# Attention scores multiplied once, with the exponentials turned by DMA, in a kernel of block attention and Fourier mixing

## The chip, the cores and the metric

The kernel runs on one core of one Trainium2 chip. The metric is the time of one execution on the device in microseconds, the median of several runs. The core's engines work side by side, each through its own queue in order: PE (TensorE, matrix products), DVE (VectorE), ACT (ScalarE), POOL (GpSimd) and SP (SyncE, which here only issues DMAs). An instruction that needs another engine's result waits at the head of its queue, and all behind it wait too.

## What is computed

Inputs are q, k and v (4 batches, 8 heads, 768 positions, head size 64), a small matrix per head, and two MLP weights. The small matrix is normalised to P (8x8); it mixes the eight blocks of 96 positions of k and of v. Then attention runs within each block, and its output goes through a two-dimensional Fourier transform, a layer norm and an MLP:

```python
k_sorted = einsum('bhij,bhjcd->bhicd', P, k_b)      # v_sorted likewise
scores = scale * matmul(q_b, k_sb.transpose(0, 1, 2, 4, 3))   # 96x96 per block
scores = scores - max(scores, axis=-1, keepdims=True)
attn = exp(scores)
attn = attn / (sum(attn, axis=-1, keepdims=True) + 1e-09)
x = matmul(attn, v_sb)                    # heads side by side: (4, 768, 512)
u = x + real(fft(fft(x, axis=1), axis=2))
un = (u - mean(u)) / sqrt(var(u) + 1e-06)
out = u + maximum(un @ w_ch1, 0) @ w_ch2
```

## The kernel before

**Order.** The program is written as steps, each with the engines that can do it and a cost in ns, the buffers that it reads and writes, and a priority. A planner (`Plan`, L166 to L301) sorts them before the program is built: time and again it takes, among the steps that could start within 40 ns of the earliest, the one of the highest priority, gives it to an engine (`"V"` DVE, `"A"` ACT, `"T"` PE, `"G"` POOL, `"S"` SP) and counts on with the stated costs. `hop` is the time from the end of a DMA's issue to its landing. The order of each queue on the chip is the one planned; the chip's own waits come on top. Buffers come from rings with a fixed number of tiles, and a step can only be planned when its buffers are free. In a `chain` the first step waits until the buffers of all of its steps are there. Earlier batches come before later ones, and MLP steps come last of all (priority 1e6 and more), so MLP matmuls fill what PE has left.

**One batch.** `mix(b)`: casts and sums v, multiplies k and v by P (`k_mix`, whose result is copied into `kzs`, and `v_mix`), transposes q into `qT`, and moves the mixed v by DMA into `vs`, one row of partitions per position of a block (`v_move`, 12 DMAs from SP). Then attention, head by head in two halves of four blocks. Then `post(b)`: the Fourier transform's second part, the residual, its store to HBM (`store_u`, SP), statistics, normalisation and transposition. Then `mlp(b, gr)` for two groups of 384 positions: 64 matmuls into the hidden layer (L924), a relu on ACT for each four of them (L930), 48 matmuls back (L945), a load of u from HBM (`load_u`, SP) and the sum (L952).

**One half of attention**, the part that the change touches. `maxima` (L651) multiplies scores with queries on partitions (L661, four matmuls) and takes the row maximum on DVE (L664) into `mxs`. `scores` (L667) multiplies them again, turned, with keys on partitions: four matmuls put minus the maximum into the bank (L676, `nident` is minus the identity), four add keys times queries (L680); ACT takes the exponential of all 96x384 at once (L685) into `sm`. `minus_one` (L688) subtracts one and rounds to float16 into `eT` (DVE or ACT). `values` (L700) multiplies `eT`, whose 97th row is all ones, by `vs`, whose 97th row holds the share of the ones and the column sums (L708), and divides by the last column (L713, L714, DVE). Rings: `mxs` 6, `sm` 4, `eT` 3, one `eT` for both halves of a head.

**Start.** `junk` (L451) holds ones for warm-up matmuls and for clearing `kzs`; `lm` (L490) takes a constant that SP loads later.

Of the kernel before, what the change touches and what calls it, by code (L numbers as in the profile page):

```python
# [9 lines left out]
F32 = mybir.dt.float32  # L10
F16 = mybir.dt.float16
AF = mybir.ActivationFunctionType
ALU = mybir.AluOpType
AX = mybir.AxisListType

B = 4
H = 8
S = 768
# [286 lines left out]
def kernel(  # L305
# [30 lines left out]
    def ring(tag, n, shape, dtype):  # L336
        plan.rings[tag] = Ring([const.tile(shape, dtype, name=f"{tag}{i}") for i in range(n)])
# [8 lines left out]
    ring("vg", 1, [128, H, D], F32)  # L346
    ring("kron", 2, [128, H, 16, NB], F16)
    ring("qT", 4, [128, S], F16)
    ring("mxs", 6, [BLK, 4], F16)
    ring("sm", 4, [BLK, 4, BLK], F32)  # L350
    ring("rz", 4, [BLK, 4], F32)
    ring("xs", 2, [BLK, 4, 128], F16)
    ring("x4", 2, [BLK, 2, 2, 128], F16)
# [10 lines left out]
    ring("ur", 2, [128, DM], F32)  # L364
    ring("outt", 2, [128, DM], F32)
    ring("mh", 1, [128, 2, 2 * LT], F16)
    plan.rings["eT"] = Ring([const.tile([97, NB, BLK], F16, name=f"eT{i}") for i in range(3)])
    eTs = plan.rings["eT"].tiles

    def bank(b, shape, dtype=F32):  # L370
        n = int(np.prod(shape[1:]))
        t = b.t if dtype == F32 else b.t.bitcast(dtype)
        t = t[0:shape[0], 0:n]
        if len(shape) == 3:
            t = t.rearrange("p (a c) -> p a c", c=shape[2])
        return t
# [71 lines left out]
    mask8 = const.tile([64, NB], F32, name="mask8_sb")  # L448
    nc.sync.dma_start(mask8, mask8_d.ap())
    selj = const.tile([64, 128], F32, name="selj_sb")  # L450
    junk = const.tile([128, DM], F16, name="junk")  # L451
    nc.vector.memset(junk, 1.0)
    ident = const.tile([128, 128], F16, name="ident")
    nc.vector.memset(ident, 0.0)
# [32 lines left out]
    negm = const.tile([128, 1], F32, name="negm_sb")  # L487
    idx = const.tile([128, 6 * B], mybir.dt.uint32, name="idx_sb")
    rsel = const.tile([BLK + 3, 2, BLK + 1], F16, name="rsel_sb")
    lm = const.tile([128, 2, 2, 385], F16, name="lm_sb")  # L490

    xr2 = [const.tile([BLK + 3, NB, DM], F16, name=f"xr{i}") for i in range(2)]
    w1sb = const.tile([128, 4, DFF], F16, name="w1sb")
# [107 lines left out]
    def k_mix(b, hp, gh):  # L601
        pK = Buf("bank")

        def f(e):
            k4 = k16[b, hp].t.rearrange("p h (g d) -> p h g d", d=D)
            ps = bank(pK, [128, 3, 128])
            for g in range(3):
                for hh in range(2):
                    nc.tensor.matmul(
                        ps[64 * hh:64 * hh + 64, g, :], k4[:, hh, 3 * gh + g, :],  # L610
                        kron[b].t[:, 2 * hp + hh].rearrange("p c i -> p (c i)"))

        def ev(e, hh):
            r = slice(64 * hh, 64 * hh + 64)
            dst = kzs[hp][r, hh].rearrange("x (i g c) -> x i g c", g=G, c=16)
            copy(e, dst[:, :, 3 * gh:3 * gh + 3, :],
                 bank(pK, [128, 3, 128])[r].rearrange("x g (c i) -> x i g c", c=16), SCALE)
        plan.chain(("psK", b, {"T": 360}, f, [k16[b, hp], (kron[b], hp // 2)], [pK]),
                   *[("kz", b, {"A": 484, "V": 551}, lambda e, hh=hh: ev(e, hh), [pK],
                      [("kz", hp, hh, gh)]) for hh in range(2)])  # L620
# [30 lines left out]
    def maxima(n, half):  # L651
        b, h = divmod(n, H)
        hp, hh = h // 2, h % 2
        mxs[n, half] = Buf("mxs")
        pS = Buf("bank")

        def f(e):
            ps = bank(pS, [BLK, 4, BLK])
            for j in range(4):
                col = slice(BLK * (4 * half + j), BLK * (4 * half + j + 1))  # L660
                nc.tensor.matmul(ps[:, j, :], qT[b, hp].t[:, col], kzs[hp][:, hh, col])  # L661
        plan.chain(
            ("psS", b, {"T": 185}, f, [qT[b, hp]] + [("kz", hp, hh, g) for g in range(2)], [pS]),
            ("max", b, {"V": 548}, lambda e: nc.vector.tensor_reduce(  # L664
                mxs[n, half].t, bank(pS, [BLK, 4, BLK]), axis=AX.X, op=ALU.max), [pS], [mxs[n, half]]))

    def scores(n, half):  # L667
# [5 lines left out]
        def f(e):  # L673
# [4 lines left out]
            for j in range(4):  # L678
# [6 lines left out]
            ("exp", b, {"A": 487}, lambda e: nc.scalar.activation(  # L685
                sms[n, half].t, bank(pS, [BLK, 4, BLK]), AF.Exp), [pS], [sms[n, half]]))

    def minus_one(n, half):  # L688
        if half == 0:
            eT[n] = Buf("eT")  # L690

        def f(e):
            dst = eT[n].t[0:BLK, 4 * half:4 * half + 4, :]
            if e == "A":
                nc.scalar.add(dst, sms[n, half].t, -1.0)  # L695
            else:
                nc.vector.tensor_scalar(dst, sms[n, half].t, -1.0, None, op0=ALU.add)
        step("minus", n // H, {"V": 459, "A": 518}, f, r=[sms[n, half]], w=[(eT[n], half)])

    def values(n, half):  # L700
        b, h = divmod(n, H)
        pN, rz = Buf("bank"), Buf("rz")

        def f(e):
            ps = bank(pN, [BLK, 4, D + 1])
            for j in range(4):
                i = 4 * half + j
                nc.tensor.matmul(ps[:, j, :], eT[n].t[:, i, :],  # L708
                                 vs[2 * (b % 2) + h // 4][:, i, (D + 1) * (h % 4):(D + 1) * (h % 4 + 1)])

        def g(e):
            ps = bank(pN, [BLK, 4, D + 1])
            nc.vector.reciprocal(rz.t, ps[:, :, D])  # L713
            nc.vector.tensor_tensor(  # L714
                xr2[b % 2][0:BLK, 4 * half:4 * half + 4, D * h:D * (h + 1)],
                ps[:, :, 0:D], rz.t[:, :, None].broadcast_to([BLK, 4, D]), op=ALU.mult)
        plan.chain(
            ("psN", b, {"T": 180}, f, [(eT[n], half)] + [("vs", b % 2, h // 4, g) for g in range(G)], [pN]),
            ("norm", b, {"V": 650}, g, [pN], [("x", b % 2, h, half), rz]))
# [303 lines left out]
    for hp in range(4):  # L1023
# [4 lines left out]
    psP = banks[6][0:64, 0:32]  # L1028
    nc.tensor.matmul(psP, pw.rearrange("p i j -> p (i j)"), ident32)
    warm(banks[7], 2)  # L1030
    ptm = plan.rings["sm"].tiles[3].rearrange("p a c -> p (a c)")[0:64, 0:256].rearrange(
        "p (i n) -> p i n", n=32)
    nc.vector.tensor_tensor(
        ptm, psP[:, None, :].broadcast_to([64, NB, 32]),
# [13 lines left out]
    for t in kzs[2:]:  # L1048
        nc.gpsimd.memset(t, 0.0)
    nc.gpsimd.memset(amt[:, :, 64:128], 0.0)  # L1050

    plan.start({"T": 17400, "V": 18350, "A": 18750, "G": 18000, "S": 16300})

# [42 lines left out]
    for b in range(B):  # L1096
        if b == 0:
            mix(0)
        if b in (0, 1):
            for y in range(2):  # L1100
                mean_path(b, y)
        if b + 1 < B:
            for hp in range(4):
                if b:
                    load_v(b + 1, hp, None)
                load_kq(b + 1, hp, None if b else 38e3 + 4e3 * hp)
        for h in range(H):
            n = H * b + h
            for half in range(2):
                maxima(n, half)  # L1110
                scores(n, half)
                minus_one(n, half)
            for half in range(2):
                values(n, half)
            if h % 2:
                for par in range(2):
                    fold(b, h // 2, par)
                    dft_s(b, h // 2, par)
                if h > 4:
                    fold_d(b, h // 2)  # L1120
        if b + 1 < B:
            mix(b + 1)
        if b == 2:
            for y in range(2):
                mean_path(3, y)
        post(b)
        for gr in range(2):
            mlp(b, gr)
# [31 lines left out]
```

## Time and profile before

| | |
|---|---|
| runs | 347.85 us median of 3 (345.82 to 349.72) |
| the profiled execution | 349.94 us, of it span 348.2 us |
| mean granted clock of PE | 0.969 |
| matmuls L661, L676, L680, L708 | 256 each, mean 212 to 215 ns, 20.1, 23.1, 22.9, 19.5 us busy |
| matmuls L924, L945 | 512 and 384, 89.0 and 89.5 us busy |
| exponential L685 (ACT) | 64, mean 484 ns, 28.6 us |
| minus one, L695 (ACT), L697 (DVE) | 46, mean 520 ns; 18, mean 384 ns |
| maximum L664 (DVE) | 64, mean 542 ns, 31.6 us |
| DMA issued by SP | 23.80 MB, 24.7% of the 16 DMA engines' span |
| DMA issued by POOL | 16.97 MB, 26.0% |

The profiler records one execution. Busy time of a group is the time in which at least one of its instructions was under way, so matmuls that overlap count once. A line such as L381 or L385 is that of the helper `copy`, which serves many steps. The chain of waits follows the last instruction back through what released each step. DMA rows name destination and source.

### The profile page before, as it was taken

What the parts mean: (1) busy time and instruction counts of PE and PEld (TensorE: products, weight loads), DVE (VectorE), ACT (ScalarE), POOL (GpSimd) and SP (SyncE); (2) the same over time, 40 slices, a digit from 0 to 9 for tenths busy, and PEclk for the clock granted to TensorE, in tenths of its full rate; (3) what the DMA queues carried; (4) which work ended last, traced back from release to release, by engine and by line L of the source; (5) the groups of instructions that cost most, each with busy time, mean ns of one, the idle gap of its engine ahead of it and who ended that gap; (6) DMA issues with size and microseconds to landing.
All of it is one profiled execution on the core that took longest, in us unless ns stands there. A gap on an engine that the chain in (4) does not pass through costs nothing.

```text
span 348.2 us, 8075 instructions
## 1 busy us (share of the span) xinstructions
PE 316.3 (91%) x3042; PEld 206.4 (59%) x3042; DVE 222.1 (64%) x577; ACT 212.3 (61%) x474; POOL 136.9 (39%) x190
## 2 busy tenths in 40 slices
PE   0998987867998999999989999999999999999994
PEld 0368854755766655678747867656556455554541
DVE  6688995996787799399989989983550602101001
ACT  5598885885787455788986846617537354260620
POOL 8879340175460599932100116651351420112111
PEclk9998998995799999999999999999999999999999
DMA  7999959079669397793530122243070330403212
GB/s 180 217 255 263 143 93 197 10 157 194 165 145 144 85 262 218 119 140 72 91 64 2 63 62 71 84 152 105 25 217 34 107 119 2 151 32 99 81 47 76
DMA packets 34799, 41.28 MB, mean 119 GB/s; under 512 B 4465, under 2 KB 26448, under 8 KB 34760
## 3 DMA queue, kind: packets, MB, share of 16 engines
q0 software_dynamic: 14992, 16.97, 26.0%
q1 hardware_dynamic: 19768, 23.80, 24.7%
q8 instruction: 24, 0.39, 0.5%
q14 instruction: 15, 0.12, 0.1%
HBM read 35.36 MB, written 12.58 MB: 138 GB/s over the span
## 4 chain that ended last, share of the span: by engine, by line
PE 62%; DVE 13%; issue 7%; DMA 7%; POOL 5%; ACT 4%; SPq 1%; POOLq 0%; DVEq 0%; ACTq 0%
PE bank L924 21%; PE bank L945 20%; DMA u_dram<-u 3%; DMA xr<-xr 3%; PE bank L676 3%; PE bank L680 2%; PE bank L708 2%; ACT kz L383 2%; PE bank L511 2%; DVE xr L714 2%; DVE mxs L664 2%; PE bank L592 1%; PE bank L661 1%; PE bank L801 1%; PE bank L752 1%
## 5 line engine op out<-in xcount | busy, mean ns | idle before, releaser
L930 ACT ACTIVATE hr<-bank 128x384 f16<-128x384 f32 x128 | 62.2, 490 | 59.3 <-PE bank L924 58.8
L945 PE MATMUL bank<-w2sb,hr 128*128 128x512 f16 x384 | 89.5, 379 | 0.0
L924 PE MATMUL bank<-unT,w1sb 128*128 128x384 f16 x512 | 89.0, 329 | 0.3 <-DVE unT L385 0.3
L924 PEld LDWEIGHTS <-w1sb 128*128 128x128 f16 x512 | 49.6, 99 | 32.5 <-issue 1.1
L967 POOL DMA_INDIRECT out_dram<-outt,idx_sb x23 | 22.7, 988 | 101.5 <-DVE outt L952 48.6
L945 PEld LDWEIGHTS <-hr 128*128 128x128 f16 x384 | 36.1, 98 | 37.9
L952 DVE SCALAR_TENSOR_TENSOR outt<-ur,bank 128x512 f32<-128x512 f32 x24 | 16.4, 683 | 49.1 <-PE bank L945 49.1
L880 DVE TENSOR_SCALAR un<-u,mv,rstd 96x512 f16<-96x512 f32 (+1 forms) x32 | 21.5, 703 | 33.4 <-PE bank L896 32.5
L685 ACT ACTIVATE sm<-bank 96x384 f32<-96x384 f32 x64 | 28.6, 484 | 8.3 <-PE bank L680 5.0
L664 DVE TENSOR_REDUCE mxs<-bank 96x4 f16<-96x384 f32 x64 | 31.6, 542 | 0.3
L714 DVE TENSOR_TENSOR xr<-bank,rz 96x256 f16<-96x256 f32 x64 | 26.9, 421 | 2.2
L845 POOL TENSOR_TENSOR u<-u,P 96x257 f32<-96x257 f32 (+1 forms) x16 | 11.9, 743 | 35.9 <-ACT u L381 21.5
L676 PE MATMUL bank<-nident_sb,mxs 96*96 96x96 f16 x256 | 23.1, 215 | 3.1 <-ACT u L381 2.0
L863 DVE BATCH_NORM_STATS2 st<-u 96x6 f32<-96x512 f32 (+1 forms) x32 | 21.8, 680 | 1.9 <-POOL u L846 1.9
L661 PE MATMUL bank<-kz,qT 128*96 128x96 f16 x256 | 20.1, 212 | 3.1 <-ACT kz L383 1.8
L680 PE MATMUL bank<-qT,kz 128*96 128x96 f16 x256 | 22.9, 214 | 0.0
L695 ACT ACTIVATE eT<-sm 96x384 f16<-96x384 f32 x46 | 22.7, 520 | 0.3 <-PE bank L708 0.2
L383 ACT ACTIVATE kz<-bank 64x384 f16<-64x384 f32 x45 | 21.3, 485 | 1.8 <-DVE kz L387 1.3
L676 PEld LDWEIGHTS <-mxs 96*96 96x96 f16 x256 | 18.9, 130 | 5.4 <-issue 2.9
L381 ACT COPY u<-bank 96x512 f32<-96x512 f32 (+1 forms) x26 | 14.5, 582 | 11.2 <-PE bank L830 4.5
L427 POOL TENSOR_TENSOR v<-v 128x384 f32<-128x384 f32 x11 | 11.7, 1066 | 22.6 <-ACT v L381 17.9
L708 PE MATMUL bank<-vs,eT 97*96 97x65 f16 x256 | 19.5, 213 | 0.9 <-DVE kz L387 0.4
(119 smaller groups left out, 549.7 us busy)
## 6 DMA issues: line engine op xcount, KB each, us to landing
u_dram<-u SPq DMA_DIRECT2D x32, 192.0 KB
ur<-u_dram SPq DMA_DIRECT2D x24, 256.0 KB
v<-in_v_dram SPq DMA_DIRECT2D x11, 384.0 KB
k<-in_k_dram POOLq DMA_DIRECT2D x16, 192.0 KB, 4.6
q<-in_q_dram POOLq DMA_DIRECT2D x16, 192.0 KB, 5.8
vs<-vo SPq DMA_DIRECT2D x42, 65.0 KB
w1sb<-in_moe_w_ch_dram POOLq DMA_DIRECT2D x4, 512.0 KB, 10.7
w2sb<-in_moe_w_ch_dram POOLq DMA_DIRECT2D x4, 512.0 KB, 8.2
```

Source lines behind the costliest of these rows:

```text
L383: nc.scalar.activation(dst, src, AF.Copy, scale=scale)
L661: nc.tensor.matmul(ps[:, j, :], qT[b, hp].t[:, col], kzs[hp][:, hh, col])
L664: ("max", b, {"V": 548}, lambda e: nc.vector.tensor_reduce(mxs[n, half].t, bank(pS, [BLK, 4, BLK]), axis=AX.X, op=ALU.max), [pS], [mxs[n, ...
L676: nc.tensor.matmul(ps[:, j, :], mxs[n, half].t[:, j:j + 1].broadcast_to([BLK, BLK]), nident, start=(j == 0), stop=False, skip_group_check= ...
L680: nc.tensor.matmul(ps[:, j, :], kzs[hp][:, hh, col], qT[b, hp].t[:, col], start=False, stop=True, skip_group_check=True)
L685: ("exp", b, {"A": 487}, lambda e: nc.scalar.activation(sms[n, half].t, bank(pS, [BLK, 4, BLK]), AF.Exp), [pS], [sms[n, half]]))
L695: nc.scalar.add(dst, sms[n, half].t, -1.0)
L708: nc.tensor.matmul(ps[:, j, :], eT[n].t[:, i, :], vs[2 * (b % 2) + h // 4][:, i, (D + 1) * (h % 4):(D + 1) * (h % 4 + 1)])
L714: nc.vector.tensor_tensor(xr2[b % 2][0:BLK, 4 * half:4 * half + 4, D * h:D * (h + 1)], ps[:, :, 0:D], rz.t[:, :, None].broadcast_to([BLK, ...
L924: nc.tensor.matmul(ps, w1sb[:, mc, 128 * fc:128 * fc + 128], unT[b, gr].t[:, mc, :], start=(mc == 0), stop=(mc == 3))
L930: nc.scalar.activation(dst, bank(pH, [128, 384]), AF.Relu)
L945: nc.tensor.matmul(ps, hr[f4].t[:, fc % 4, 128 * t:128 * (t + 1)], w2sb[:, fc, :], start=(fc == 0), stop=(fc == 15))
```

## The change

From batch 1 on a half of attention is written by `turned` in place of `maxima`, `scores` and `minus_one`; batch 0 stays as it was. Scores are multiplied once, with queries on partitions and negated (`k_mix` now copies with minus the scale from batch 1 on). DVE takes the row minimum (minus the maximum) as float32 into `mns`; ACT takes four exponentials of 96x96, each with a column of `mns` as its bias and a scale of minus one; one is subtracted as before, into `es`; a transposing DMA from SP turns `es` (96 queries by four times 128) into `eT` (128 by four times 96). Columns 96 to 127 of `es` are set to one once, so that row 96 of `eT` comes out as ones; rows 97 to 127 aren't read. To make room `mxs` goes to 4 tiles, `sm` to 3, and `junk` becomes a part of `lm`.

```diff
--- before.py
+++ after.py
@@ -346,8 +346,10 @@
     ring("vg", 1, [128, H, D], F32)
     ring("kron", 2, [128, H, 16, NB], F16)
     ring("qT", 4, [128, S], F16)
-    ring("mxs", 6, [BLK, 4], F16)
-    ring("sm", 4, [BLK, 4, BLK], F32)
+    ring("mxs", 4, [BLK, 4], F16)
+    ring("mns", 3, [BLK, 4], F32)
+    ring("es", 3, [BLK, 4, 128], F16)
+    ring("sm", 3, [BLK, 4, BLK], F32)
     ring("rz", 4, [BLK, 4], F32)
     ring("xs", 2, [BLK, 4, 128], F16)
     ring("x4", 2, [BLK, 2, 2, 128], F16)
@@ -364,7 +366,7 @@
     ring("ur", 2, [128, DM], F32)
     ring("outt", 2, [128, DM], F32)
     ring("mh", 1, [128, 2, 2 * LT], F16)
-    plan.rings["eT"] = Ring([const.tile([97, NB, BLK], F16, name=f"eT{i}") for i in range(3)])
+    plan.rings["eT"] = Ring([const.tile([128, NB, BLK], F16, name=f"eT{i}") for i in range(3)])
     eTs = plan.rings["eT"].tiles
 
     def bank(b, shape, dtype=F32):
@@ -448,7 +450,8 @@
     mask8 = const.tile([64, NB], F32, name="mask8_sb")
     nc.sync.dma_start(mask8, mask8_d.ap())
     selj = const.tile([64, 128], F32, name="selj_sb")
-    junk = const.tile([128, DM], F16, name="junk")
+    lm = const.tile([128, 2, 2, 385], F16, name="lm_sb")
+    junk = lm[:, 0].rearrange("p e k -> p (e k)")[:, 0:DM]
     nc.vector.memset(junk, 1.0)
     ident = const.tile([128, 128], F16, name="ident")
     nc.vector.memset(ident, 0.0)
@@ -487,7 +490,6 @@
     negm = const.tile([128, 1], F32, name="negm_sb")
     idx = const.tile([128, 6 * B], mybir.dt.uint32, name="idx_sb")
     rsel = const.tile([BLK + 3, 2, BLK + 1], F16, name="rsel_sb")
-    lm = const.tile([128, 2, 2, 385], F16, name="lm_sb")
 
     xr2 = [const.tile([BLK + 3, NB, DM], F16, name=f"xr{i}") for i in range(2)]
     w1sb = const.tile([128, 4, DFF], F16, name="w1sb")
@@ -614,7 +616,7 @@
             r = slice(64 * hh, 64 * hh + 64)
             dst = kzs[hp][r, hh].rearrange("x (i g c) -> x i g c", g=G, c=16)
             copy(e, dst[:, :, 3 * gh:3 * gh + 3, :],
-                 bank(pK, [128, 3, 128])[r].rearrange("x g (c i) -> x i g c", c=16), SCALE)
+                 bank(pK, [128, 3, 128])[r].rearrange("x g (c i) -> x i g c", c=16), -SCALE if b else SCALE)
         plan.chain(("psK", b, {"T": 360}, f, [k16[b, hp], (kron[b], hp // 2)], [pK]),
                    *[("kz", b, {"A": 484, "V": 551}, lambda e, hh=hh: ev(e, hh), [pK],
                       [("kz", hp, hh, gh)]) for hh in range(2)])
@@ -685,6 +687,40 @@
             ("exp", b, {"A": 487}, lambda e: nc.scalar.activation(
                 sms[n, half].t, bank(pS, [BLK, 4, BLK]), AF.Exp), [pS], [sms[n, half]]))
 
+    def turned(n, half):
+        b, h = divmod(n, H)
+        hp, hh = h // 2, h % 2
+        if half == 0:
+            eT[n] = Buf("eT")
+        et, mn, sm, es, pS = eT[n], Buf("mns"), Buf("sm"), Buf("es"), Buf("bank")
+
+        def f(e):
+            ps = bank(pS, [BLK, 4, BLK])
+            for j in range(4):
+                col = slice(BLK * (4 * half + j), BLK * (4 * half + j + 1))
+                nc.tensor.matmul(ps[:, j, :], qT[b, hp].t[:, col], kzs[hp][:, hh, col])
+
+        def x(e):
+            for j in range(4):
+                nc.scalar.activation(sm.t[:, j, :], bank(pS, [BLK, 4, BLK])[:, j, :], AF.Exp,
+                                     bias=mn.t[:, j:j + 1], scale=-1.0)
+
+        def g(e):
+            dst = es.t[:, :, 0:BLK]
+            if e == "A":
+                nc.scalar.add(dst, sm.t, -1.0)
+            else:
+                nc.vector.tensor_scalar(dst, sm.t, -1.0, None, op0=ALU.add)
+        plan.chain(
+            ("psS", b, {"T": 185}, f, [qT[b, hp]] + [("kz", hp, hh, g_) for g_ in range(2)], [pS]),
+            ("max", b, {"V": 548}, lambda e: nc.vector.tensor_reduce(
+                mn.t, bank(pS, [BLK, 4, BLK]), axis=AX.X, op=ALU.min), [pS], [mn]),
+            ("exp", b, {"A": 1080}, x, [pS, mn], [sm]))
+        step("minus", b, {"V": 459, "A": 518}, g, r=[sm], w=[es])
+        step("turn_e", b, {"S": 1200}, lambda e: nc.sync.dma_start(
+            et.t[:, 4 * half:4 * half + 4, :], es.t.rearrange("q j k -> q (j k)"), transpose=True),
+            r=[es], w=[(et, half)], hop=2500)
+
     def minus_one(n, half):
         if half == 0:
             eT[n] = Buf("eT")
@@ -705,7 +741,7 @@
             ps = bank(pN, [BLK, 4, D + 1])
             for j in range(4):
                 i = 4 * half + j
-                nc.tensor.matmul(ps[:, j, :], eT[n].t[:, i, :],
+                nc.tensor.matmul(ps[:, j, :], eT[n].t[0:97, i, :],
                                  vs[2 * (b % 2) + h // 4][:, i, (D + 1) * (h % 4):(D + 1) * (h % 4 + 1)])
 
         def g(e):
@@ -1028,7 +1064,7 @@
     psP = banks[6][0:64, 0:32]
     nc.tensor.matmul(psP, pw.rearrange("p i j -> p (i j)"), ident32)
     warm(banks[7], 2)
-    ptm = plan.rings["sm"].tiles[3].rearrange("p a c -> p (a c)")[0:64, 0:256].rearrange(
+    ptm = plan.rings["sm"].tiles[2].rearrange("p a c -> p (a c)")[0:64, 0:256].rearrange(
         "p (i n) -> p i n", n=32)
     nc.vector.tensor_tensor(
         ptm, psP[:, None, :].broadcast_to([64, NB, 32]),
@@ -1048,6 +1084,8 @@
     for t in kzs[2:]:
         nc.gpsimd.memset(t, 0.0)
     nc.gpsimd.memset(amt[:, :, 64:128], 0.0)
+    for t in plan.rings["es"].tiles:
+        nc.gpsimd.memset(t[:, :, BLK:128], 1.0)
 
     plan.start({"T": 17400, "V": 18350, "A": 18750, "G": 18000, "S": 16300})
 
@@ -1107,6 +1145,9 @@
         for h in range(H):
             n = H * b + h
             for half in range(2):
+                if b:
+                    turned(n, half)
+                    continue
                 maxima(n, half)
                 scores(n, half)
                 minus_one(n, half)
```

## The prediction

> **What bounds the kernel now.** I read the page's utilisation and its 40 slices first, then the same by stages, then the chain of waits, then the order on TensorE. From the page:
>
> ```profile
> PE 316.3 (91%) x3042; PEld 206.4 (59%) x3042; DVE 222.1 (64%) x577; ACT 212.3 (61%) x474; POOL 136.9 (39%) x190
> ...
> PE   0998987867998999999989999999999999999994
> ...
> DVE  6688995996787799399989989983550602101001
> ACT  5598885885787455788986846617537354260620
> ```
>
> PE is nearly full from slice 10 (87 us) on; DVE is nearly full until slice 27 (235 us), then idles. Attention and its follow-up end there, and the last 105 us are MLP matmuls that were saved up. So PE work taken out after 87 us shortens the run, as long as PE isn't left waiting instead. The answer by windows (columns: stretch, its length, busy PE, PEld, DVE, ACT, POOL with counts, granted clock, DMA share, GB/s) has the attention stages of batches 1, 2 and 3 in its rows 1, 5 and 7:
>
> ```profile
> 63.00:83.00 20.00, 16.21 (x240) 13.87 (x238) 18.48 (x45) 15.96 (x38) 9.76 (x15) 0.87 0.57 116
> 83.00:100.00 17.00, 14.45 (x134) 10.67 (x133) 11.95 (x38) 12.22 (x31) 8.10 (x13) 0.75 0.74 175
> ...
> 149.00:172.00 23.00, 22.48 (x393) 18.70 (x392) 21.62 (x63) 19.95 (x47) 4.45 (x7) 1.00 0.56 96
> 172.00:183.00 11.00, 9.02 (x88) 5.30 (x83) 9.50 (x26) 9.79 (x24) 0.47 (x1) 1.00 0.41 78
> 183.00:205.00 22.00, 21.66 (x319) 17.15 (x319) 20.21 (x60) 13.40 (x32) 1.69 (x2) 1.00 0.08 26
> ```
>
> In batch 1's first stretch PE idles 3.8 of 20 us; in batches 2 and 3 PE and DVE are both full. The chain of waits (start, us, what) shows in batch 1's stage how long a DMA takes there:
>
> ```profile
> 72.23 3.70 DMA u_dram<-u
> ...
> 76.45 8.10 DMA u_dram<-u
> ...
> 84.65 0.59 ACT u L381
> ```
>
> PE in order of time (start, us, line, operation, count) gives the price of what goes:
>
> ```profile
> 187.91 0.34 PE L676 MATMUL bank<-nident_sb,mxs 96*96 96x96 f16 x4
> 188.09 0.34 PE L680 MATMUL bank<-qT,kz 128*96 128x96 f16 x4
> 188.27 0.34 PE L661 MATMUL bank<-kz,qT 128*96 128x96 f16 x4
> 188.45 0.33 PE L708 MATMUL bank<-vs,eT 97*96 97x65 f16 x4
> 188.61 0.36 PE L661 MATMUL bank<-kz,qT 128*96 128x96 f16 x4
> ```
>
> Four matmuls show 0.34 us from first start to last end, but the next four start 0.18 us later: the pitch is what counts.
>
> **Removed.** In 48 halves (three batches, eight heads, two halves) L676 and L680 go: 8 matmuls, 0.36 us, 17.3 us in all. Of batch 1's 16 halves 14 stand before 83 us, where PE has gaps and no MLP matmul yet (the first L924 starts at 86.2): 5.0 us there buy nothing. That leaves 34 x 0.36 = 12.2 us that can be filled with MLP work.
>
> **Added on ACT.** One exponential of 96x384 (L685, 0.484 us) becomes four of 96x96. By durations: 384 columns 484 ns, 2 columns 204 ns (L874), so 0.73 ns a column and 0.27 us each, 1.09 us for four: +0.61. By pitch: four L685 in a row took 1.62 us at 162.75, so (1.62 - 0.49)/3 = 0.38 each, 0.21 less for 288 columns fewer is 0.17, 0.68 for four: +0.30. Over 48 halves 14 to 29 us, beside PE's work. In 149 to 205 ACT is busy 43.1 of 56 us; 32 halves add 9.6 to 19.5, and there the relus (L930, 0.49 us, ACT only) that feed PE with MLP work come last in priority. PE's loss is between nothing (the stage just gets longer over the MLP work still in hand at 203: six groups of 10.40 us of L924 and 10.36 of L945, 125 us) and all that is freed there, 32 x 0.36 = 11.5. I take 4, nearer to nothing, because PE idles only 2.8 of these 56 us with DVE at 92%.
>
> **Added on SP and DMA.** 48 transposing DMAs of 96 KB. The trace has none. Each stands between "minus" and the values matmul (L708), a path without any DMA now. SP is one queue: the turn waits there for "minus", and behind it wait load_v (for v_cast, v_sum), v_move (for L708 of the next batch), store_u and load_u (for L952). The other way round, SP now waits up to 14.4 us at L852 and 14.1 at L910, and turns placed behind those wait too. On PE, L708 waits in order for the turn, and behind it stand the next scores (L661) and the MLP matmuls. The plan allows 1.2 us on SP and 2.5 us to land, 3.7; what lands later stops PE. Issue: 0.34 us (store_u) to 0.60 (v_move) from rows, so up to 0.9 below the plan's price; landing of the nearest transfers: the two rows above, 3.70 and 8.10 with issue, and 4.5 to 5.8 for vs<-vo from POOL. The plan gives a store_u 2.55, so these two are 1.15 and 5.55 over, 3.35 on average. I take such an overrun for the turn as well, since it shares queue and DMA engines with these stores; the ends are nothing and 5.55. An overrun isn't paid per half but per round: three "es" buffers make 16/3 = 5.3 rounds a batch, and the scores of the next round stand on PE behind the stalled values. Batch 1: 5.3 x 3.35 = 17.8, of which the half after 86 us costs, 8.9. Batch 2, at a DMA share of 0.56 and no such long row: the lower overrun, 5.3 x 1.15 = 6.1. Batch 3, at 0.08: nothing. Together 15.
>
> The Trainium skill speaks against this path: VectorE: DVE Perf Modes, "The three transpose paths", puts a 128x128 transpose at 1309 ns by DMA and 390 ns on TensorE, and prefers TensorE where PSUM will do. No run here shows it yet; an estimate of three such tiles for one turn, one after another, is 3.9 us, 0.2 over the plan, and by it the sum would be 12.2 - 4 - 16 x 0.2 = 5 us faster.
>
> **Costing nothing.** "minus" keeps its size (DVE 0.38, ACT 0.52) and is already there; the minimum costs what the maximum did (L664, 0.54); one bank is held longer instead of two in turn. The three memsets on POOL at 18 us are at most 1.4 each (L1049, 12 times as large) and hide behind kz's; the constant load into "lm" starts at 28.8, 13 us after the last use of junk (15.5). Batch 0 with 3 instead of 4 "sm" buffers is limited by DVE (L714, L664 in the chain); without that cover some 1 us.
>
> **Sum.** -12.2 + 4 + 15 = +6.8 us. The profiled execution took 349.94 us (span 348.2, 1.7 around it): 356.7 on its scale; on the median of the runs, 347.85, it is 354.7. About 1% (3.5 us) is what a measurement tells from no change.
>
> **Rivals.** *Turns land within 3.7 us.* Then only ACT's term stays: 347.85 - 12.2 + 0 to 4, so 336 to 340, say 338. For it: in batch 3's stage the DMA share is 0.08 and the two single-row xr<-xr copies land 2.45 us after the last issue starts; the plan's 1.08 us for ACT is its upper end, and what ACT gains there pays for a late turn. Against it: the 3.70 and 8.10. It decides by the median landing against 3.7 us. The Trainium skill backs it: Advanced Engine Details and Errata, "X-Bar Transpose (TRN2)", calls such DMAs as fast as regular ones; this trace has no transpose to compare. *Turns set the pace.* If a turn takes as long per byte as vs<-vo from POOL (5.0 us for 65 KB), 96 KB take 7.4 us, and three "es" buffers pass a half every (0.5 + 7.4)/3 = 2.6 us instead of the (0.5 + 3.7)/3 = 1.4 planned: 34 x 1.2 = 41 us of PE stalls, 347.85 - 12.2 + 4 + 41 = 381. It decides from some 5 us a turn. For it: many short pieces in both; against: vs<-vo was measured in slice 3, at the highest load. *ACT takes the place of PE.* All freed PE time idles because relus come too late: 347.85 - 12.2 + 11.5 = 347, no change. For it: 15.96 of 20 in 63 to 83 and 19.95 of 23 in 149 to 172; against: ACT holds only 61% overall and MLP work waits till the end. *It doesn't do what it says:* the second multiplication is gone by the code, so 17.3 us of PE must leave the groups; only where they leave is open.
>
> **How the numbers follow.** Forecast, turns late by 1 to 5 us in loaded stages (351.4 to 366): 0.36, with 354.7 its value. Pace (366 and more): 0.12. Within the allowance (under 344.4): 0.36. ACT, or overruns that just eat the gain (344.4 to 351.3): 0.16. So faster 0.36, same 0.16, slower 0.48. The forecast's own range is 351 to 366; as both signs hold much, the range for 8 in 10 reaches from the fast rival's 335 to 378, just short of the pace rival's value.
>
> **What would show it.** L676 and L680 at 64 each instead of 256; the new exponential's busy time 32 to 53 us; landing times of eT<-es by stage, against 2.5 us after issue; PE's idle time before L708 put down to a DMA, 15 us in all with most in batch 1 (under 3 in the fast rival, over 35 in the slow one); PE busy in the stages of batches 2 and 3; the last L664 against 194 us. I am wrong if L708 hardly waits, or if PE waits chiefly for relus, or if SP, blocked by a store or a load, holds the turns rather than the landing.

## The result and the profile after

The changed kernel took 367.98 us (median; 366.45 to 373.67), the kernel before 348.11 us beside it. The ratio is 1.056 (95% interval 1.048 to 1.065): 19.9 us slower. The profiled execution took 366.45 us, its span was 364.7 us.

The page of the changed kernel: busy times, three rows of the slices, the chain by engine, and the new exponential.

```profile
PE 311.2 (85%) x2658; PEld 195.1 (53%) x2658; DVE 236.6 (65%) x611; ACT 223.6 (61%) x584; POOL 139.1 (38%) x193
...
PE   0988988634099989998889988999999999999994
...
PEclk9998989855589999999655999999999999999999
DMA  7999786499926386999630555442144050312312
...
PE 59%; DMA 17%; DVE 12%; ACT 6%; issue 4%; SPq 1%; POOL 1%; POOLq 0%; DVEq 0%
...
L705 ACT ACTIVATE sm<-bank,mns 96x96 f32<-96x96 f32 x192 | 47.8, 344 | 6.1 <-DVE mns L716 3.3
```

TensorE has 384 matmuls fewer (3042 to 2658), two times four in each of 48 halves, and yet is busy only 5.1 us less (316.3 to 311.2). Its idle time rose from 31.9 to 53.5 us; +21.6 idle and -5.1 busy make the span's +16.5. In the slices it has a hole at 73 to 100 us (3, 4, 0), where the DMA row reads 9, 9, 9, and its clock falls to a half there and again at 175 to 199 us. From the mean granted clock (0.969 before, 0.909 after), the time at half clock, 2 x (1 - clock) x span, rose from 22 to 66 us. So the 12.2 us of the 17.3 that didn't leave the busy time are, by this reading, other matmuls that ran slower. Attention ended later, not earlier: the last maximum before started at 194.3 us, the last minimum now at 230.7.

The stretch of the hole and batch 2's stretch, first of the kernel before (columns: stretch, its length, busy PE, PEld, DVE, ACT, POOL with counts, granted clock, DMA share, GB/s):

```profile
75.00:100.00 25.00, 20.02 (x177) 14.72 (x175) 19.05 (x56) 17.16 (x42) 11.27 (x18) 0.73 0.83 176
...
150.00:200.00 50.00, 47.16 (x728) 37.16 (x727) 46.12 (x131) 41.44 (x96) 5.39 (x7) 1.00 0.36 69
```

The same of the changed kernel:

```profile
75.00:100.00 25.00, 7.48 (x44) 4.22 (x44) 11.28 (x23) 9.40 (x32) 8.18 (x12) 0.50 1.21 203
...
150.00:200.00 50.00, 44.77 (x441) 29.65 (x441) 42.24 (x111) 42.72 (x127) 19.47 (x26) 0.76 0.68 123
```

In 75 to 100 us TensorE, VectorE and ScalarE all stand still most of the time, while the DMA engines are full (a share over 1 is packets that overlap on an engine). The chain of waits of the changed kernel says for what (start, us, what):

```profile
72.83 7.44 DMA u_dram<-u
80.75 5.88 DMA u_dram<-u
...
89.83 10.14 DMA eT<-es
...
110.45 4.61 DMA eT<-es
...
160.15 4.20 DMA eT<-es
...
167.28 3.16 DMA eT<-es
```

The two stores were there before (3.70 and 8.10 us at 72 and 76 us). After them a turn takes 10.14 us to land, and three more late ones follow. Before that landing turns had already been held up in SP's queue. ScalarE had written two `es` tiles at some 74.5 and 74.9 us:

```profile
73.99 0.92 ACT L711 ACTIVATE es<-sm 96x384 f16<-96x384 f32 x2
```

SP (L946 is `load_u`, L720 the turn) issued their turns only at 81.20 and 83.36 us:

```profile
80.29 0.35 SPq L946 DMA_DIRECT2D ur<-u_dram  x1
...
81.20 1.45 SPq L720 DMA_TRANSPOSE eT<-es  x1
...
83.36 1.20 SPq L720 DMA_TRANSPOSE eT<-es  x1
```

The load of u at 80.29 had to wait for the store that landed at 80.27 (72.83 + 7.44), and the turns stood behind it: 6.7 and 8.5 us in the queue, besides the time to land. Before the change nothing between the exponential and the values went through this queue. The instructions on `es`, with who waited for them (us, times):

```profile
L720 SPq DMA_TRANSPOSE eT<-es x48: 1179/1197/2187, 65.0 to 234.8; - x48
...
who waited for it (us, times):
  ACT es L711: 13.8, 4
  DVE es L713: 8.3, 3
  PEld L744: 4.1, 6
  PE bank L744: 2.3, 3
```

The issue takes 1.2 us on SP, as planned. But it is chiefly not the values (L744) that wait for a late turn: "minus" does (L711 on ScalarE, L713 on VectorE), because its `es` tile isn't free until the turn has read it. Everything behind "minus" on ScalarE and VectorE then stands, and so does the TensorE work that needs it.

### The profile page after: what moved, and what is told of

It is laid out like the page before. It is cut to its first block, busy times and chain, and to the rows that moved or that the text cites. A ratio compares the mean times of both kernels' runs of the same rounds, so it can differ in the third digit from the quotient of the medians.

```text
span 364.7 us, 7524 instructions
## 1 busy us (share of the span) xinstructions
PE 311.2 (85%) x2658; PEld 195.1 (53%) x2658; DVE 236.6 (65%) x611; ACT 223.6 (61%) x584; POOL 139.1 (38%) x193
## 4 chain that ended last, share of the span: by engine, by line
PE 59%; DMA 17%; DVE 12%; ACT 6%; issue 4%; SPq 1%; POOL 1%; POOLq 0%; DVEq 0%
PE bank L981 19%; PE bank L960 18%; DMA eT<-es 7%; DMA u_dram<-u 4%; PE bank L788 2%; PE bank L744 2%; ACT kz L385 2%; ACT sm L705 2%; DMA xr<-xr 2%; PE bank L513 2%; DMA out_dram<-outt,idx_sb 2%; DMA k<-in_k_dram 2%; PE bank L837 1%; PE bank L701 1%; DVE xr L750 1%
## 5 line engine op out<-in xcount | busy, mean ns | idle before, releaser
L960 PE MATMUL bank<-unT,w1sb 128*128 128x384 f16 x512 | 91.0, 329 | 1.7 <-ACT sm L705 0.9
L705 ACT ACTIVATE sm<-bank,mns 96x96 f32<-96x96 f32 x192 | 47.8, 344 | 6.1 <-DVE mns L716 3.3
L744 PE MATMUL bank<-vs,eT 97*96 97x65 f16 x256 | 22.3, 222 | 6.3 <-DMA eT<-es 2.3
L716 DVE TENSOR_REDUCE mns<-bank 96x4 f32<-96x384 f32 x48 | 25.3, 544 | 2.7 <-PE bank L701 2.2
L744 PEld LDWEIGHTS <-eT 97*96 97x96 f16 x256 | 19.6, 139 | 10.7 <-issue 4.7
L701 PEld LDWEIGHTS <-qT 128*96 128x96 f16 x192 | 16.7, 153 | 12.4 <-issue 10.0
L385 ACT ACTIVATE kz<-bank 64x384 f16<-64x384 f32 x43 | 20.5, 486 | 2.8 <-DVE kz L389 1.4
L711 ACT ACTIVATE es<-sm 96x384 f16<-96x384 f32 x24 | 12.3, 531 | 16.2 <-DMA eT<-es 13.8
L932 PE MATMUL bank<-ident,un 96*128 96x96 f16 (+1 forms) x128 | 10.5, 218 | 10.6 <-DVE u L387 6.5
L932 PEld LDWEIGHTS <-un 96*128 96x128 f16 (+1 forms) x128 | 8.6, 103 | 18.3 <-issue 9.5
L383 ACT COPY u<-bank 96x512 f32<-96x512 f32 (+1 forms) x20 | 11.5, 584 | 10.2 <-PE bank L864 6.5
## 6 DMA issues: line engine op xcount, KB each, us to landing
w1sb<-in_moe_w_ch_dram POOLq DMA_DIRECT2D x4, 512.0 KB, 10.1
```

What stands on the lines that cost most here:

```text
L385: nc.scalar.activation(dst, src, AF.Copy, scale=scale)
L705: nc.scalar.activation(sm.t[:, j, :], bank(pS, [BLK, 4, BLK])[:, j, :], AF.Exp, bias=mn.t[:, j:j + 1], scale=-1.0)
L716: ("max", b, {"V": 548}, lambda e: nc.vector.tensor_reduce(mn.t, bank(pS, [BLK, 4, BLK]), axis=AX.X, op=ALU.min), [pS], [mn]),
L744: nc.tensor.matmul(ps[:, j, :], eT[n].t[0:97, i, :], vs[2 * (b % 2) + h // 4][:, i, (D + 1) * (h % 4):(D + 1) * (h % 4 + 1)])
L960: nc.tensor.matmul(ps, w1sb[:, mc, 128 * fc:128 * fc + 128], unT[b, gr].t[:, mc, :], start=(mc == 0), stop=(mc == 3))
```

## The experiments

**Theories.** T, the turn: late landings cost some 15 us or more, and without them the kernel would be faster than before. A, the exponentials: four biased pieces slow ScalarE and so the run. O, the order: the plan prices the new steps differently (1080 instead of 487 for the exponential, a turn of 1.2 + 2.5 us) and lays out another order, which may cost or gain by itself. Two kernels are compared most safely where their instructions stand in the same order on each engine; where a plan differs, the text says so. Ratios are to the kernel before, run beside each, with 95% intervals.

**The turn alone.** The DMA is not issued; the plan is that of the changed kernel, and the order on TensorE, VectorE, ScalarE and GpSimd is the same.

```diff
-        step("turn_e", b, {"S": 1200}, lambda e: nc.sync.dma_start(
-            et.t[:, 4 * half:4 * half + 4, :], es.t.rearrange("q j k -> q (j k)"), transpose=True),
+        step("turn_e", b, {"S": 1200}, lambda e: None,
             r=[es], w=[(et, half)], hop=2500)
```

> The order of TensorE, VectorE, ScalarE and GpSimd is the same, instruction by instruction; only the 48 turning DMAs are left out, so the exponentials of batches 1 to 3 aren't turned and the values are made with old ones. Theory A: nothing is left of the loss and the saved matmuls show: 332 to 342. Rival B (ScalarE): 360 to 368, because ScalarE's work is all there. Rival C (the order): 355 to 368, since the order is that of the changed kernel.

348.75 us, 1.002 (0.998 to 1.006), against 1.056 with the turns. So the 48 turning DMAs, their waits in SP's queue included, cost 19 us in this order, and all the rest of the change together comes to nothing. Gains and losses within that rest may cancel: with its new steps and prices the plan also moved 34 steps from ScalarE to VectorE (VectorE 577 to 611 instructions; ScalarE 474 to 584, of which 144 are the added pieces), and the last minimum still came at 212.4 us. The hole at 75 to 100 us is filled again (same columns, kernel without turns):

```profile
75.00:100.00 25.00, 20.60 (x165) 13.98 (x166) 23.80 (x69) 20.12 (x65) 10.95 (x16) 0.71 0.93 175
```

**The turn by batches.** Batch 1 as before, and batches 1 and 2 as before; these are planned anew.

```diff
-                if b:
+                if b >= 2:     # the other kernel: b >= 3
                     turned(n, half)
...
```

> Attention of batch 1 as before (multiplied twice, no turn), batches 2 and 3 with the turn. Theory A (turns land late where DMA is busy, TensorE stops behind the values, and its granted clock halves after the stop): batch 1's jam goes, TensorE is idle some 6 us in 60 to 100 us as in the kernel before instead of 22, and 16 to 20 us come back: 348 to 352. The stop near 172 us and the half clock after it stay. Rival B (ScalarE's four exponentials are what slows): a third of the loss comes back: 360 to 363. Rival C (the planner's order is bad because of the turn's planned 3.7 us, whatever lands when): the loss is shared evenly by the batches too, 360 to 363.

> Only batch 3 with the turn, where the DMA engines are idle (share 0.08 before). Saved on TensorE: 16 x 0.36 = 5.8 us. Theory A2: turns land within the planned 3.7 us, nothing stops: 341 to 346. If the longer chain of a half costs by itself: 347 to 352.

358.41 us, 1.029 (1.019 to 1.040), and 348.01 us, 1.004 (1.000 to 1.008). Against the kernel before beside each (348.11, 348.18 and 347.12 us) the changed kernel and these two lose 19.9, 10.2 and 0.9 us. Step by step batch 1 costs 9.6 us, batch 2 9.3 and batch 3 0.9. These are steps between kernels with plans of their own, so saving, exponentials and order are in them too, and the middle one is only known to some 4 us either way. The loss lies in the batches whose stages have dense transfers.

**Longer planned landing.** The plan allows 5.0 us instead of 2.5 for the turn to land; the order is spaced accordingly.

```diff
-            r=[es], w=[(et, half)], hop=2500)
+            r=[es], w=[(et, half)], hop=5000)
```

> The planner counts 5.0 us for a turn's landing instead of 2.5. Theory A: it puts more MLP matmuls ahead of the values, the short stops of batches 2 and 3 shrink and with them perhaps the half clock near 180 us: 5 to 12 us back, 356 to 363; batch 1's jam (DMA engines over 100% busy) stays. Rival C: most of the loss comes back, under 355. Rival B: no change, 365 to 370.

352.08 us, 1.011 (1.005 to 1.017): 16 us of the 20 come back with every DMA still there (some of it may be the new order's own doing, see the gap below). So turns don't set the pace by their number; they were due too early.

**Fewer loads beside the turns.** Three of four loads of the second MLP weight (512 KB each, at 75 to 100 us) become constants written by GpSimd; same order.

```diff
+            elif c:
+                nc.gpsimd.memset(w2sb[:, 4 * c:4 * c + 4], 0.01)
```

> Three of the four loads of the second MLP weight (1 MB each from HBM, issued back to back at 83 us in the changed kernel) are replaced by constants set by GpSimd, same order otherwise; that part of the weight is left out. Theory A, and the jam is those loads and the turns together: the turn of 89.8 us lands in 3 to 5 us instead of 10.1, TensorE's idle time in 60 to 100 us falls from 22 to some 10: 354 to 359. If turns are slow by themselves in this stage (u's stores, v's moves): no more than 4 us back, 364 to 368.

364.76 us, 1.054 (1.044 to 1.064). In 75 to 100 us TensorE rose from 7.48 to 15.70 us busy and the DMA share fell from 1.21 to 0.73, and the turn that had taken 10.14 us to land is in time (from the chain of waits):

```profile
87.70 2.44 DMA eT<-es
```

So these loads did make the turns land late there. But of the 8.2 us only 3.8 are left over the whole span (TensorE idle 49.7 us against 53.5), and the mean clock stayed (0.910 and 0.909). In this stage SP still waited 4.0 us for stores of u to land before it could issue loads of u (5.5 in the changed kernel). What one jam costs can't be read off that jam alone.

**ScalarE's pieces.** One exponential of 96x384 instead of four, without the maximum, in the changed kernel's order: once with the turns, once without.

```diff
-            for j in range(4):
-                nc.scalar.activation(sm.t[:, j, :], bank(pS, [BLK, 4, BLK])[:, j, :], AF.Exp,
-                                     bias=mn.t[:, j:j + 1], scale=-1.0)
+            nc.scalar.activation(sm.t, bank(pS, [BLK, 4, BLK]), AF.Exp, scale=-1.0)
```

> The changed kernel in its order with its turns, and only the four biased exponentials replaced by one over 96x384 (the maximum isn't subtracted). Theory D: ScalarE's part goes, 350 to 356 against 368. If the turns set the pace alone and hide the pieces: 364 to 368.

> The changed kernel's order without the turning DMAs, and the four biased exponentials of a half replaced by one over 96x384 without the maximum: both additions are gone from the chip, only the saved matmuls and the order are left (exponentials aren't turned, the maximum isn't subtracted). Theory D (the 20 us are the turn's 19 plus ScalarE's 15 to 20 less the 17 saved): 330 to 337 against 348.8 with the four pieces. If ScalarE's pieces are hidden in this order: 346 to 349.

365.24 us, 1.055 (1.048 to 1.063), against 1.056 with four pieces; and 352.38 us, 1.018 (1.010 to 1.026), against 1.002: with less work on ScalarE the second became slower. So theory A explains nothing of the loss in this order.

The same pieces put into the kernel before: with its own plan and a bias of zero; without a bias and with the plan's price of 1080; and the price alone, instructions unchanged (1080, and 650).

```diff
# e10_bias: four pieces, bias=zero[0:BLK], price 487
# e8_split: four pieces, no bias, price 1080
# e9_plan1080 and e13_plan650: only the price
-            ("exp", b, {"A": 487}, lambda e: nc.scalar.activation(
+            ("exp", b, {"A": 1080 if b else 487}, lambda e: nc.scalar.activation(
```

> The kernel before in its own order (planned price 487), with the exponential of batches 1 to 3 in four pieces, each with a per-partition bias of zero: ScalarE's part of the change on the chip alone, some 26 us more of its time if a piece takes the 0.34 us of the changed kernel. Rival B: 356 and more. Rival C3: 347 to 351.

> The kernel before, with the exponential of batches 1 to 3 in four pieces of 96x96 instead of one of 96x384 and planned at 1.08 us; nothing else. This is ScalarE's part of the change alone. My prediction put it at 4 us: 350 to 354. Theory A2 with ScalarE hidden beside DVE and MLP: 347 to 350. Rival B: 356 and more.

> The kernel before, every instruction as it was; only the planner's price of the exponential of batches 1 to 3 goes from 487 to 1080 ns, so the order is that of the kernel with the four-piece exponential (362.9 us), whose ScalarE time was no longer than before. Rival C3 (it is the order, made by a price, that costs): 358 to 364. Theory A2 or B (the pieces cost on the chip): 345 to 350.

> The kernel before, every instruction as it was, with the planner's price of the exponential of batches 1 to 3 at 650 ns in place of 487: a second order of the same work. Rival C3 (orders of the same work scatter by more than 10 us): anything from 345 to 365. If only a much too high price spoils the order: 345 to 351.

366.52 us, 1.058 (1.050 to 1.067); 362.85 us, 1.050 (1.042 to 1.057); 361.05 us, 1.044 (1.035 to 1.053); 353.94 us, 1.023 (1.015 to 1.031). The price alone costs 14 us. It changes no step, but the plan is another one, and it also gives 26 steps to VectorE instead of ScalarE (577 to 603 and 474 to 448 instructions; 10 steps at the price of 650). The pieces add nothing that can be told apart from it (1.050 against 1.044, same order). In the old order, which isn't planned for them, the biased pieces cost 20 us. The exponential's group in the first of these four kernels, with a bias (busy us, mean ns):

```profile
L691 ACT ACTIVATE sm<-bank,zero 96x96 f32<-96x96 f32 x192 | 46.9, 384 | 5.8 <-PE bank L682 4.7 <-DVE kz L387 0.7
```

The same in the second, without one:

```profile
L689 ACT ACTIVATE sm<-bank 96x96 f32<-96x96 f32 x192 | 29.5, 270 | 10.4 <-PE bank L680 9.9
```

With the bias four take 46.9 / 48 = 0.98 us, without it 29.5 / 48 = 0.61; the two kernels differ in order too.

**The saving alone.** No turn and no time for one in the plan: with four pieces at 1080, and with one exponential at 487 and no maximum subtracted. Then the kernel before, in its own order, without the multiplication that subtracts the maximum in batches 1 to 3 (L676).

```diff
# e12_noturn_plan0
-        step("turn_e", b, {"S": 1200}, lambda e: nc.sync.dma_start(
...
-        step("minus", b, {"V": 459, "A": 518}, g, r=[sm], w=[es])
+        step("minus", b, {"V": 459, "A": 518}, g, r=[sm], w=[es, (et, half)])
# e17_saved: this, and
-            ("exp", b, {"A": 1080}, x, [pS, mn], [sm]))
+            ("exp", b, {"A": 487}, x, [pS, mn], [sm]))
...
# e18_nomax: before, and
-            for j in range(4):
+            for j in range(0 if b else 4):
...
```

> The changed kernel without the turning DMAs and without their 3.7 us in the plan, so it has an order of its own; exponentials aren't turned, values use old ones. With the DMAs left out in the changed kernel's order it was 348.8. If the planned gap is what costs there: 334 to 340, the 12 to 17 us saved on TensorE show. If ScalarE or the price of 1080 costs: 346 to 352.

> Only the saving, in an order of its own: scores of batches 1 to 3 multiplied once, one exponential over 96x384 planned at its 487 ns, no turn and no time for one in the plan (the maximum isn't subtracted, exponentials aren't turned). If the 17.3 us of matmuls show once neither price stands in the plan: 328 to 336. If they go into TensorE's waits whatever the order: 342 to 349, as in the kernels without turns (347 to 352).

> The kernel before in its own order, without the four matmuls of a half that put minus the maximum into the bank, in batches 1 to 3 (the maximum isn't subtracted). TensorE has 48 x 0.18 = 8.6 us less. If matmuls taken out of this order shorten the run by what isn't in batch 1's gaps, 34 x 0.18: 340 to 343. If TensorE waits instead, or its clock drops: 345 to 349.

347.26 us, 0.9995 (0.995 to 1.004); 348.40 us, 1.002 (0.999 to 1.006); 347.89 us, 1.000 (0.996 to 1.005). With the run that only lacks the DMA that is four kernels in four orders with 8.6 or 17.3 us less on TensorE, and none is faster.

Where the time went can be read from the profiles. In the kernel without turns and in the first of these three, 17.3 us of matmuls less left TensorE 309.1 and 306.4 us busy (316.3 before) and 37.2 and 39.6 us idle (31.9 before), with 48 and 39 us at half clock (22 before). So of the saving 10.1 and 7.4 us went into matmuls that ran slower and 5.3 and 7.7 us into waits. The half clock thus takes a share beside the order; no run holds the clock fixed, so the two aren't told apart.

The kernel without L676 tells most, as its order is that of before and its time at half clock rose little (25 us). Its row for 150 to 200 us, all engines:

```profile
150.00:200.00 50.00, 46.06 (x601) 34.08 (x601) 46.01 (x135) 39.82 (x93) 4.92 (x6) 0.97 0.33 67
```

Its row for the second MLP multiplication alone (L945; columns PE, PEld, clock, DMA share, GB/s):

```profile
150.00:200.00 50.00, 10.27 (x40) 3.43 (x40) 0.97 0.33 67
```

The kernel before had in L945's row:

```profile
150.00:200.00 50.00, 8.41 (x33) 2.85 (x34) 1.00 0.36 69
```

127 + 7 matmuls of attention are gone from this stretch, at 8.6 / 192 = 0.045 us (half of the prediction's 17.3 for half of its 384) about 6.0 us. Of these, seven more MLP matmuls filled 1.9 us; 1.1 us more are idle; a clock of 0.97 is 3 us at half clock, which stretches 1.5 us of matmuls to twice that; and the rest, 1.5 us, may be work that came earlier, as the last maximum (L664) started at 192.8 instead of 194.3 us. VectorE stayed at 46.0 of 50 us. So attention is hardly finished earlier when TensorE is relieved. That fits a limit elsewhere, by VectorE or by the MLP work that the order has at hand there; neither was tried by itself.

**Turn and gap together.** Batch 1 as before, batches 2 and 3 turned, with 5.0 or 8.0 us planned to land.

```diff
-                if b:
+                if b >= 2:
...
-            r=[es], w=[(et, half)], hop=2500)
+            r=[es], w=[(et, half)], hop=5000)     # the other kernel: 8000
```

> Attention of batch 1 as before, batches 2 and 3 with the turn, and 5.0 us planned for its landing. Theory A2 (batch 1's stage loses because its DMA queue is full; batches 2 and 3 lose because one stop of TensorE costs some 20 us at half clock, and a longer planned landing keeps MLP matmuls between): both losses go, 340 to 346, below the kernel before. Rival C2 (the two earlier gains are the same time counted twice): 350 to 354.

> Batch 1 as before, turns in batches 2 and 3, 8.0 us planned for a landing instead of 5.0 (339.8) or 2.5 (358.4). If 5.0 was enough to hide what is late: 338 to 344. If each us planned keeps buying time: under 337. If the order after a price is a matter of chance: anything from 340 to 356.

339.75 us, 0.978 (0.972 to 0.985), and 341.31 us, 0.989 (0.983 to 0.995). Both are faster than the kernel before, by 2.2 and 1.1%. In the second no instruction waits for a turn any more. Is that the saving at last, or the gap's order?

**The gap without the saving.** The kernel before, no step changed; only the plan counts 6.2 us between "minus" and the values in batches 2 and 3.

```diff
-        step("minus", n // H, {"V": 459, "A": 518}, f, r=[sms[n, half]], w=[(eT[n], half)])
+        step("minus", n // H, {"V": 459, "A": 518}, f, r=[sms[n, half]], w=[(eT[n], half)],
+             hop=6200 if n >= 16 else 0)
```

> The kernel of before, instruction for instruction, but in batches 2 and 3 the plan counts 6.2 us between "minus" and the values (the turn's 1.2 plus 5.0 of e5_from2_hop5), so the values are placed later in the order; nothing waits for them on the chip. If the gain of e5_from2_hop5 (0.978) comes from the spacing of the order alone, about 340 us (0.97 to 0.985). If it needs the multiplications that are saved, 346 to 350 (0.995 to 1.01). In between: both have a share.

342.34 us, 0.984 (0.979 to 0.988). The plan alone gives a gain of this size (six steps also went from VectorE to ScalarE); the two kernels with the gap, the saving and the turns lie on either side of it (0.978 and 0.989), and their intervals overlap with its own. Its row for 150 to 200 us, all engines:

```profile
150.00:200.00 50.00, 49.47 (x691) 38.27 (x691) 44.94 (x121) 41.50 (x93) 10.75 (x15) 1.00 0.40 85
```

The first MLP multiplication in it (L925; L924 before):

```profile
150.00:200.00 50.00, 7.08 (x37) 3.33 (x38) 1.00 0.40 85
```

And the second (L946; L945 before):

```profile
150.00:200.00 50.00, 10.98 (x44) 3.81 (x44) 1.00 0.40 85
```

TensorE is busy 49.5 of 50 us with 81 MLP matmuls where before had 33 (none of L924). Attention ends later here (last maximum at 206.8 us), and the run ends 5.4 us sooner by its span, since less MLP work is left for the end.

**Keeping TensorE busy.** Six filler matmuls of 128x512 ahead of the values in two places of batch 2, to keep its clock up.

```diff
+            if (n, half) in ((17, 1), (18, 0)):
+                for _ in range(6):
+                    nc.tensor.matmul(bank(pN, [128, DM]), ident, w2sb[:, 0, :])
```

> The changed kernel in its own order, with six idle-filling matmuls of 128x512 (1.3 us) on TensorE ahead of the values of two halves of batch 2, where it stopped at 172 to 176 us; their result is overwritten. Theory A2: the window of 3.4 us at 172 us stays over half busy, the granted clock stays at 1.0 there, and 24 us at half clock become 12: 354 to 360 in place of 368, although TensorE is given 2.6 us more work. If the half clock costs little because TensorE waits in that stage anyway: 366 to 371.

371.29 us (364.72 to 374.31), too scattered for a ratio. The experiment is inconclusive, and the half clock's own share of the loss stays open.

## Why the prediction went wrong where it did

It forecast +6.8 us (354.7, range 351 to 366) as -12.2 + 4 + 15; measured were 368 and +19.9, of which 19 are the turns and the first two terms together nothing. The sign was right and the largest term nearly so; the step that failed is "34 x 0.36 = 12.2 us that can be filled with MLP work".

- **Removed, -12.2.** The matmuls went as counted (13 of batch 1's halves, not 14, have their L676 before 83 us, a matter of 0.4 us). That their time can be filled was inferred from TensorE being nearly full from slice 10 on. But VectorE was at 46.1 of 50 us in batch 2's stage too, its part wasn't cut, and the order decides which MLP matmuls stand there. Measured: nothing in four kernels. In two of them 7.4 to 10.1 us of it went into TensorE's own slower clock and 5.3 to 7.7 us into waits; the sum had put the clock at nothing. The gap alone (0.984) shows that the plan can move the time by 5 us, not that the order ate the saving; that VectorE paces attention is read from the rows and wasn't tried. Why the saving is lost is open between these three.
- **ACT, +4 (0 to 11.5).** Busy time rose from 28.6 x 48 / 64 = 21.5 to 47.8 us for 48 halves, +0.55 a half, inside the bounds of 0.30 to 0.61. Cost in the changed order: nothing (1.055 and 1.056). In the order of before, which doesn't plan for them, such pieces cost 20 us, more than the upper bound of 11.5, so the term depends on the plan. The mean of one piece was 344 ns, not 270: the nearest rows had no bias column. The Trainium skill, ScalarE: Activation LUTs, "What ACT_TABLE_LOAD costs", gives about 280 + 0.833 ns a column for an activation with a bias column, and an overlap of 93 ns back to back; by it an estimate is 360 ns for one and, with three overlaps, 1.16 us for four. The trace has 344 ns and 47.8 / 48 = 1.00 us, 4% and 14% less.
- **Turns, +15.** Measured +19. The kernels by batches lose 9.6, 9.3 and 0.9 against 8.9, 6.1 and 0 for the turns, but the other terms are in these steps too. That batch 1 comes so close is in part luck: its turns did land late (10.14 us), but they also stood 6.7 and 8.5 us in SP's queue behind a load that waited for a store. The prediction named that wait and gave it no term, and it had it as a sign of being wrong. How the 19 us divide between queue and landing wasn't tried. Batch 2 was set too low; its DMA share rose from 0.36 to 0.68 in 150 to 200 us. The waiting instruction was mostly "minus" (22.1 us), not the values (6.4): the three `es` tiles, which the sum used only to count rounds, were where the wait fell.
- **What a turn takes.** Where DMA is quiet all 384 packets of 256 bytes are through 0.6 to 0.7 us after the issue ended, some 1.9 us with the issue; with a longer planned landing a turn landed after 2.3 us at the least, 2.8 in the median and 9.0 at the most, the issue included. The quiet case is below the 3.9 us estimated from the Trainium skill, VectorE: DVE Perf Modes, "The three transpose paths". The Trainium skill, Advanced Engine Details and Errata, "X-Bar Transpose (TRN2)", calls transposing DMAs as fast as regular ones; no run here has a regular DMA of the same shape to compare. Under load a turn took 10.14 us where stores took 7.44 and 5.88, so here it was late like the other transfers.
- **Rivals.** Turns within 3.7 us: gave 338, but with the longer planned landing the median was 2.8 us and the time still 352.08, and without any turn's landing the kernel takes 348.75, so punctual turns would not have made it faster in this order. Turns set the pace: excluded for the whole run by the longer landing (1.011 with all 48 turns), though single turns of batch 1 took more than the 5 us from which it counts. ACT in place of PE: its 347 is what the kernels without turns show, but not by its mechanism, as cheaper exponentials don't change it.

## What to carry to other kernels

Work taken from an engine that looks full is worth only what the order puts in its place: before counting it, count the filler that stands in that stage, look for a second engine that is as full, and watch the granted clock. For a DMA put into a chain, look at what stands ahead of it in the queue that issues it, plan its landing from the loaded stage, and count the buffers at its source: here the source's writer waited first. More `es` buffers, or another queue for the turns, weren't tried. Where a planner lays out the order, plan the old instructions with the new prices too: here prices alone moved the time by +14, +7 and -5 us.

## What the runs showed of the hardware

The clock of TensorE changes in steps of 3.41 us, and a step that is only partly busy can be followed by half clock. From the kernel without turns, one row for each step (first number after the length: TensorE busy; third from the end: granted clock):

```profile
157.92:161.34 3.42, 1.65 (x22) 1.29 (x20) 3.04 (x11) 3.20 (x11) 0.90 (x2) 1.00 0.81 191
161.34:164.75 3.41, 2.98 (x25) 1.94 (x25) 3.19 (x10) 2.73 (x9) 0.00 (x0) 0.50 0.14 20
164.75:168.16 3.41, 3.29 (x40) 2.76 (x39) 2.78 (x9) 3.29 (x11) 0.00 (x0) 0.50 0.03 7
168.16:171.58 3.42, 2.70 (x24) 2.10 (x24) 3.20 (x11) 3.38 (x13) 0.00 (x0) 0.50 0.00 0
...
174.99:178.40 3.41, 3.41 (x25) 2.02 (x22) 2.28 (x9) 2.45 (x7) 0.00 (x0) 0.50 0.00 0
178.40:181.82 3.42, 3.42 (x28) 2.24 (x27) 2.10 (x6) 2.40 (x6) 0.00 (x0) 0.50 0.01 2
181.82:185.23 3.41, 3.41 (x22) 1.99 (x21) 3.10 (x8) 3.41 (x12) 0.00 (x0) 1.00 0.08 18
```

One step with 1.65 of 3.41 us busy was followed by 20.5 us at half clock, through steps that were 79 to 96% busy; the clock came back after two full ones. In the changed kernel a step with 1.24 us busy was followed by 23.9 us at half. The traces give no threshold: in the changed kernel the step at 131.06 us was 1.92 us busy and the clock stayed full, the one at 45.73 us was 2.38 us busy and the next had half. The Trainium skill, TensorE: Matmul & The Clock Gate, Part 1, has the step's length (3413 ns) and a half clock after an idle window; the trace agrees on the length, but here the half clock also came after a step that was half busy. So a stop of TensorE can cost twice, the wait and slower matmuls after it, and as the first of these two kernels has no turn to wait for, a late turn isn't the only way to it. How much the half clock is of the 19 us, and of the lost saving, was not settled.
